# Loading a chunk's r, k and w as 128 rows instead of 96, and zeroing the heads of the 32 extra rows

## The chip, the cores and the metric

One core of a Trainium2 chip. The metric is the device time of one execution in microseconds (us); the kernel before took 305.26 us, the median of three executions (304.26 to 307.01).

## The reference

A recurrent attention over 768 positions (4 batches, 8 heads, head dimension 48) feeds a mixture of experts that uses one of 8 experts per token. Only the first half matters for the change:

```python
for t in range(S):
    cur = einsum('bhd,bhe->bhde', u * k[t], v[t])
    y[t] = einsum('bhd,bhde->bhe', r[t], state + cur)
    state = w[t][:, None] * state + einsum('bhd,bhe->bhde', k[t], v[t])
```

The rows of y, with the heads side by side, go through a skip test, a router (softmax over 8 logits, the best expert taken) and the chosen expert, `relu(x @ w1) @ w2`, times its gate.

## The kernel before

The positions are cut into 24 chunks of 128 (6 for each batch). A chunk works on all 8 heads: a partition holds one dimension of one of two head groups, and the free axis holds four heads of 128 positions each. A group has 48 dimensions, so the data fill 96 of the 128 partitions. Partitions 16 to 63 hold one group, 64 to 111 the other, and 0 to 15 and 112 to 127 hold nothing of the chunk.

A loop over s from -2 to 24 is a software pipeline. In step s PE finishes chunk s (`update`, `outputs`, `rows_out`) and makes the scores of chunk s+1 (`rows_of_keys`, `scores`, `bonus_sums`), DVE scans chunk s+2 (`prep_scan`, `prep_keys`, `prep_reads`) and then masks the scores of chunk s+1 and writes its bonus term into psY (`mask`, L321; `bonus`, L334), and SP issues the loads of chunk s+4. Every engine works through its instructions in the order in which they are written (`manual_schedule`). From step 3 on the experts' weights are loaded as well, and at steps 6, 12 and 18 a router pass is dripped between the DVE instructions.

The buffers of r, k and w (`wrk_sb`) go round in three, those of v transposed (`vt_sb`) in four. A load writes only 96 partitions of a buffer, so the other 32 are set once at the start: w to 1, r and k to 0 (`clear_w`, L201; `clear_rk`, L204). For buffer 0 POOL and DVE do it, for buffers 1 and 2 POOL alone.

The decay is handled by two scans on DVE: q (L266) is the product of w from a position to the end of the chunk, and rh (L288) the product from the start, which begins with a "head", 1/q of the first position. The head is written into a spare column of the w buffer by the reciprocal at L281. Then rp = r * rh (L293), kq = k * q (L283) and rk = r * k (L275). In an empty partition w = 1 and r = k = 0 make all three zero.

The constants come over ACT's DMA queue in `load_chunk(0)`: c_sb, then u_sb in three pieces (`shifted` copies the two groups from the layout of the host to partitions 64, 16 and 0), then the transposed v of chunk 0. After that ACT loads its table and clears psA, sblk and fills ubk_sb (L221 to L231). `rowsk` is 1 in the 96 used partitions and 0 in the others; it is loaded in step 18 on SP's queue, and only a test near the end of the kernel reads it.

Of the kernel before, what the change touches and what calls it, by code (L numbers as in the profile page):

```python
# [8 lines left out]
F32 = mybir.dt.float32  # L9
# [6 lines left out]
ALU = mybir.AluOpType  # L16
# [3 lines left out]
B, H, S, D = 4, 8, 768, 48  # L20
E, DM, DF = 8, 384, 1024
P = 128
# [5 lines left out]
NP = H // 2  # L28
# [12 lines left out]
R_OFF = 1 + NP * CW  # L41
K_OFF = R_OFF + NP * P
V_OFF = K_OFF + NP * P
HP = 64
LO = HP + D
KO = HP - D
# [10 lines left out]
def rwkv_moe_kernel(ctx, tc, wrk, wrk0, vN, uP, wgs, wgp, w12, cst, out):  # L57
    nc = tc.nc
# [6 lines left out]
    n = len(seq)  # L65
# [56 lines left out]
    with tc.tile_pool(name="att", bufs=2) as att, \  # L122
# [6 lines left out]
        def shifted(eng, dst, src):  # L129

            eng.dma_start(dst[HP:], src[HP:])
            eng.dma_start(dst[KO:HP], src[:D])
            eng.dma_start(dst[:KO], src[D:HP])

        def load_chunk(i):
            b, c = seq[i]
            rows = wrk[b, c].rearrange("g d n -> (g d) n")
            t = wrk_sb[i % NBUF]
            vf = vt_sb[i % (NBUF + 1)].rearrange("p a j -> p (a j)")
            if i == 0:  # L140
                nc.sync.dma_start(t[KO:LO, :R_OFF], rows[:, :R_OFF])
                nc.sync.dma_start(t[KO:LO, R_OFF:V_OFF], rows[:, R_OFF:V_OFF])
                nc.scalar.dma_start(c_sb[:, :C_IOTA], cst[:, :C_IOTA])
                shifted(nc.scalar, u_sb, uP)
                nc.scalar.dma_start(vf, wrk0[:, V_OFF:V_OFF + NP * P])
                return
            nc.sync.dma_start(t[KO:LO], rows[:, :V_OFF])
            for g in range(2):
                nc.sync.dma_start(vf[64 * g:64 * g + D], wrk[b, c, g, :, V_OFF:V_OFF + NP * P])

# [6 lines left out]
        c_sb = keep.tile([P, C_W], F32, name="c_sb")  # L157
        ubk_sb = keep.tile([P, NP, P], F32, name="ubk_sb")
        u_sb = pers.tile([P, NP], F32, name="u_sb")
        rowsk = keep.tile([P, 1], F32, name="rowsk")  # L160
        ident = c_sb[:, C_ID:C_ID + P]
        tri = c_sb[:, C_TRI:C_TRI + P]
        iota = keep.tile([P, 2 * P], BF16, name="iota")
# [36 lines left out]
        def clear_w(eng, i):  # L200
            eng.memset(wrk_sb[i][:, :R_OFF], 1.0)  # L201

        def clear_rk(eng, i):
            eng.memset(wrk_sb[i][:, R_OFF:], 0.0)  # L204

        def setup():
            clear_w(nc.gpsimd, 0)
            clear_rk(nc.vector, 0)
            load_chunk(0)
            nc.vector.memset(warm, 0.0)  # L210
            clear_w(nc.gpsimd, 1)
            clear_rk(nc.gpsimd, 1)
            nc.gpsimd.memset(vt_sb[1], 0.0)
            load_chunk(1)
            load_v(0)
            nc.vector.memset(pss, 0.0)
            ints = ones_w.bitcast(U32)
            for a in range(NP):
                at = (a + 1) * CW - 1
                nc.vector.memset(ints[:, at // 4:at // 4 + 1], 1 << 8 * (at % 4))  # L220
            nc.scalar.activation(junk0, warm[:, 0:1], AF.Exp)  # L221
            for z in (*psa, *sblk):
                nc.scalar.copy(z.rearrange(("p a j -> p (a j)", "p a g j -> p (a g j)")
                                           [len(z.shape) - 3]), warm)
            nc.gpsimd.memset(ubk_sb, 0.0)
            clear_w(nc.gpsimd, 2)
            clear_rk(nc.gpsimd, 2)
            nc.gpsimd.memset(vt_sb[2], 0.0)
            for g in range(2):
                rows = slice(64 * g, 64 * g + HP)  # L230
                nc.scalar.copy(ubk_sb[rows, :, rows],  # L231
                               u_sb[rows].rearrange("p (a o) -> p a o", o=1)
                               .to_broadcast([HP, NP, HP]))


            nc.tensor.matmul(psy.rearrange("p a j -> p (a j)"), warm[:, :P], warm,
                             start=True, stop=True, skip_group_check=True)
            nc.tensor.matmul(psu.rearrange("p a j -> p (a j)"), warm[:, :P], warm[:, :NP * HP],
                             start=True, stop=True, skip_group_check=True)
# [38 lines left out]
        def prep_keys(i):  # L278
            wk = work[i]
            heads = wk["w"][:, 0:NP * CW].rearrange("p (a j) -> p a j", a=NP)  # L280
            nc.vector.reciprocal(heads[:, :, 0:1], wk["q"][:, :, 0:1])  # L281
            kq = wk["kq"] = att.tile([P, NP, P], F32, tag="kq", name=f"kq{i}")
            nc.gpsimd.tensor_tensor(kq, wk["k"], wk["q"][:, :, 1:1 + P], op=ALU.mult)  # L283

# [288 lines left out]

        with tc.manual_schedule():
            setup()
            fill(FILL0)
            for s in range(-2, n + 1):
                on = lambda i: 0 <= i < n
                if s + 4 < n:
                    load_chunk(s + 4)  # L580
                if on(s + 3) and s + 3 >= 1:
                    load_v(s + 3)
                if s == -2:
                    nc.sync.dma_start(wgp_sb, wgp)
                if s == 1:
                    nc.sync.dma_start(c_sb[:, C_IOTA:], cst[:, C_IOTA:])
                if s == LATE:
                    nc.sync.dma_start(wgs_sb, wgs)
                    shifted(nc.sync, rowsk, cst[:, C_HS + 2:C_HS + 3])
                if on(s - 1):  # L590
                    store(s - 1)
                for i0, m in GROUPS:
                    if i0 + m == s:
                        pace[0] = 1 if i0 + m < LATE else 2
                        later.append(router(i0, m))
                        if i0 + m == LATE:
                            later.append(early())
                if on(s):
                    update(s)
                    carry(s)  # L600
                if on(s + 2):
                    prep_scan(s + 2)
                drip(pace[0])
                if on(s):
                    outputs(s)
                flush()
                if on(s + 2):
                    prep_keys(s + 2)
                    drip(pace[0])
                    if s != -1:  # L610
                        prep_reads(s + 2)
                if s == -2:
                    bonus_keys(0)
                    nc.gpsimd.memset(vt_sb[3], 0.0)
                    nc.gpsimd.memset(onesb, 1.0)
                    nc.gpsimd.memset(ohs, 0.0)
                    nc.gpsimd.memset(key, 0.5)
                if on(s):
                    evict(s)
                if on(s + 1):  # L620
                    rows_of_keys(s + 1)
                    if s == 0:
                        bonus_sums(1)
                    scores(s + 1)
                    drip(2 * pace[0])
                    mask(s + 1, 0)
                    mask(s + 1, 1)
                    drip(pace[0])
                    if s != 0:
                        bonus_sums(s + 1)  # L630
                    bonus(s + 1)
                if s == -1:
                    prep_reads(1)
                if on(s + 2):
                    prep_check(s + 2)
                for _ in range(min(2, len(marks))):
                    marks.popleft()()
                if s == n - 1:
                    early_tokens(0)
                if on(s):  # L640
                    rows_out(s)
                flush()
                if s in (1, 2, 3):
                    nc.scalar.copy(*((trib, tri), (identb, ident),
                                     (iota, c_sb[:, C_IOTA:C_IOTA + 2 * P]))[s - 1])
                if s == 4:
                    nc.scalar.copy(iotaw, iota.bitcast(F32))
                k = s + 1 - W_AT
                for eq, k0 in (((0, 1), 0), ((1, 0), 9), ((0, 0), 16), ((1, 1), 18)):
                    if k == k0:  # L650
                        gens[eq] = load_weights(*eq)
                    if k0 <= k < k0 + 3:
                        next(gens[eq])
                if 3 <= k < 9:
                    split_slice(0, 3 + k, nc.gpsimd)
                if 12 <= k < 18:
                    split_slice(1, k - 12, nc.gpsimd)
# [40 lines left out]
    with tc.tile_pool(name="wset1", bufs=1) as ws1, tc.tile_pool(name="moe", bufs=2) as moe:  # L698
# [55 lines left out]

        def verdict():
            psf = ps1.tile([P, 512], F32, tag="psT", name="psf", bufs=2)
            nc.tensor.matmul(psf[0:1, 0:1], rowsk, vt[:, 0:1], start=True, stop=False)
            nc.tensor.matmul(psf[0:1, 0:1], rows1_, vt[:, 3:4], start=False, stop=True)
            nc.vector.tensor_scalar(flag_i, psf[0:1, 0:1], 0.0, None, op0=ALU.is_gt)

# [245 lines left out]
```

## Time and profile before

| | |
|---|---|
| median of three executions | 305.26 us (304.26 to 307.01) |
| the profiled execution | 304.25 us, of which the span from first to last instruction is 302.5 us |
| PE busy | 289.8 us, 96% of the span |
| DVE, ACT, POOL busy | 216.8, 176.2, 141.3 us |
| mean granted TensorE clock | 0.995 |
| loads of r, k, w after the first chunk | 23 of 579.4 KB |

The profile is of one execution. The DMA share of a stretch is the mean busy share of the 16 DMA engines; a value of 1 or a little more means that they always had a packet in hand.

### The profile page before, as it was taken

What the parts mean: (1) busy time and instruction counts of PE and PEld (TensorE: products, weight loads), DVE (VectorE), ACT (ScalarE), POOL (GpSimd) and SP (SyncE); (2) the same over time, 40 slices, a digit from 0 to 9 for tenths busy, and PEclk for the clock granted to TensorE, in tenths of its full rate; (3) what the DMA queues carried; (4) which work ended last, traced back from release to release, by engine and by line L of the source; (5) the groups of instructions that cost most, each with busy time, mean ns of one, the idle gap of its engine ahead of it and who ended that gap; (6) DMA issues with size and microseconds to landing.
All of it is one profiled execution on the core that took longest, in us unless ns stands there. A gap on an engine that the chain in (4) does not pass through costs nothing.

```text
span 302.5 us, 8272 instructions
## 1 busy us (share of the span) xinstructions
PE 289.8 (96%) x3228; PEld 269.3 (89%) x3228; DVE 216.8 (72%) x410; ACT 176.2 (58%) x493; POOL 141.3 (47%) x140
## 2 busy tenths in 40 slices
PE   6799999999999999899999999999999999999993
PEld 2689889889888988799899999999999999999992
DVE  5987779877888787976253879693967859496320
ACT  5284645799577986797433666391846638184310
POOL 7795665978976589766106771302011020201101
PEclk9999999999999999999999999999999999999998
DMA  6999999999799967765513699746266563630001
GB/s 189 261 243 262 286 282 245 237 249 223 194 289 265 284 181 225 191 224 165 176 72 89 195 378 362 254 168 229 101 226 227 208 250 103 246 117 26 9 2 40
DMA packets 22737, 60.28 MB, mean 199 GB/s; under 512 B 3926, under 2 KB 10490, under 8 KB 22688
## 3 DMA queue, kind: packets, MB, share of 16 engines
q1 hardware_dynamic: 20176, 53.79, 60.5%
q0 software_dynamic: 2048, 5.48, 5.5%
q8 instruction: 27, 0.44, 0.6%
q10 hardware_dynamic: 464, 0.40, 0.6%
q14 instruction: 22, 0.18, 0.2%
HBM read 52.60 MB, written 7.86 MB: 200 GB/s over the span
## 4 chain that ended last, share of the span: by engine, by line
issue 32%; PE 23%; DVE 5%; POOL 5%; DMA 4%; ACT 1%; POOLq 1%; SPq 0%; DVEq 0%
POOL out L728 5%; PE psY L370 3%; PE psY L365 3%; PE psB L330 3%; PE psA L315 3%; PE psX L381 2%; PE psH L115 2%; DMA vt<-wrk 2%; DMA v<-vN 1%; PE psu L344 1%; DMA xg<-out,idr 1%; DVE psY L334 1%; PE psH L792 1%; PE psH L791 1%; PE psH L790 1%
## 5 line engine op out<-in xcount | busy, mean ns | idle before, releaser
L728 POOL DMA_INDIRECT out<-fin,ids x16 | 17.1, 1070 | 100.9 <-DVE fin L823 94.4
L797 ACT ACTIVATE hh<-psH 128x256 fp32r<-128x256 f32 x60 | 23.1, 384 | 56.8 <-PE psH L792 53.8
L792 PE MATMUL psH<-xTh,w1l 128*128 128x256 f32 x168 | 47.5, 283 | 0.0
L791 PE MATMUL psH<-xTl,w1h 128*128 128x256 f32 x168 | 47.5, 283 | 0.0
L790 PE MATMUL psH<-xTh,w1h 128*128 128x256 f32 x168 | 47.5, 283 | 0.0
L321 DVE TENSOR_TENSOR asb<-psA,c_sb 128x512 f32<-128x512 f32 x48 | 30.8, 684 | 17.0 <-PE psA L315 17.0
L814 PE MATMUL psO<-w2h,hh 128*128 128x384 f32 x120 | 40.9, 341 | 0.0
L816 PE MATMUL psO<-w2h,hl 128*128 128x384 f32 x120 | 40.2, 335 | 0.0
L815 PE MATMUL psO<-w2l,hh 128*128 128x384 f32 x120 | 40.1, 334 | 0.0
L802 DVE SCALAR_TENSOR_TENSOR hl<-psH,hh 128x256 fp32r<-128x256 f32 x60 | 25.2, 421 | 12.3 <-ACT hh L797 12.0
L275 POOL TENSOR_TENSOR rk<-wrk 128x512 f32<-128x512 f32 x24 | 30.9, 1287 | 6.2 <-POOL rp L293 2.5
L288 DVE TENSOR_TENSOR_SCAN rh<-wrk,pss 128x520 f32<-128x520 f32 x24 | 29.7, 1235 | 4.2 <-PE pss L498 2.4
L792 PEld LDWEIGHTS psH<-xTh,w1l 128*128 128x128 f32 x168 | 32.2, 192 | 0.0
L791 PEld LDWEIGHTS psH<-xTl,w1h 128*128 128x128 f32 x168 | 32.2, 192 | 0.0
L790 PEld LDWEIGHTS psH<-xTh,w1h 128*128 128x128 f32 x168 | 32.2, 191 | 0.0
L293 POOL TENSOR_TENSOR rp<-wrk,rh 128x512 f32<-128x512 f32 x23 | 27.2, 1182 | 9.8 <-DVE rh L288 7.9
L283 POOL TENSOR_TENSOR kq<-wrk,q 128x512 f32<-128x512 f32 x24 | 28.3, 1179 | 7.3 <-DVE q L266 5.9
L266 DVE TENSOR_TENSOR_SCAN q<-wrk,pss 128x520 f32<-128x520 f32 x24 | 29.3, 1222 | 2.0 <-DMA wrk<-wrk 1.9
L90 DVE TENSOR_TENSOR w2l<-r,w2h 128x512 fp32r<-128x512 f32 x42 | 27.8, 687 | 1.0
L365 PE MATMUL psY<-asb,v 128*48 128x128 f32 x384 | 26.6, 276 | 1.8 <-DVE psY L334 1.3
L89 ACT CAST w2h<-r 128x512 fp32r<-128x512 f32 x48 | 27.9, 626 | 0.4 <-DMA r<-w 0.4
L330 PE MATMUL psB<-rk,ubk_sb 128*128 128x128 f32 x192 | 27.7, 287 | 0.0
(148 smaller groups left out, 633.7 us busy)
## 6 DMA issues: line engine op xcount, KB each, us to landing
r<-w SPq DMA_DIRECT2D x48, 512.0 KB, 5.4
wrk<-wrk SPq DMA_DIRECT2D x23, 579.4 KB, 7.0
v<-vN SPq DMA_DIRECT2D x24, 192.0 KB, 5.6
out<-x SPq DMA_DIRECT2D x24, 192.0 KB, 4.9
vt<-wrk SPq DMA_DIRECT2D x46, 96.0 KB, 6.4
wrk<-wrk SPq DMA_DIRECT2D x1, 384.0 KB, 4.7
vt<-wrk ACTq DMA_DIRECT2D x1, 256.0 KB, 7.7
out<-fin,ids POOLq DMA_INDIRECT x16, 4.1
```

The source lines that it names most:

```text
L275: nc.gpsimd.tensor_tensor(work[i]["rk"].rearrange("p a j -> p (a j)"), t[:, R_OFF:K_OFF], t[:, K_OFF:V_OFF], op=ALU.mult)
L288: nc.vector.tensor_tensor_scan(rh.rearrange("p a j -> p (a j)"), wk["w"][:, 0:NP * CW], ones_at[:, :NP * CW], 1.0, op0=ALU.mult, op1=ALU.max)
L321: nc.vector.tensor_tensor(s, psa[g], tri.rearrange("p (o j) -> p o j", o=1).to_broadcast([P, NP, P]), op=ALU.mult)
L330: nc.tensor.matmul(wk["psb"][:, a], ubk_sb[:, a], wk["rk"][:, a], start=True, stop=True)
L365: nc.tensor.matmul(psy[64 * g:64 * g + D, a], v[:, 2 * a + g], wk["asb"][g][:, a], start=False, stop=(c == 0), skip_group_check=True)
L728: sc = nc.gpsimd.indirect_dma_start(out=out, out_offset=bass.IndirectOffsetOnAxis(ap=ids[:, s % 2, s // 2:s // 2 + 1], axis=0), in_=o, in_ ...
L790: nc.tensor.matmul(ps, w1h[:, o:o + P], xTh[:, kc], start=(kc == 0), stop=False)
L791: nc.tensor.matmul(ps, w1h[:, o:o + P], xTl[:, kc], start=False, stop=False)
L792: nc.tensor.matmul(ps, w1l[:, o:o + P], xTh[:, kc], start=False, stop=(kc == KC - 1))
L814: nc.tensor.matmul(pso, h[j, fc][0], w2h[:, o], start=(fc == 0), stop=False)
L815: nc.tensor.matmul(pso, h[j, fc][0], w2l[:, o], start=False, stop=False)
L816: nc.tensor.matmul(pso, h[j, fc][1], w2h[:, o], start=False, stop=(fc == FC - 1))
```

## The change

The rows of all chunks lie one after another in DRAM, so the load of chunk i, for i from 1 to 22, now takes 128 rows that start 16 rows before its own: the 32 outer partitions receive the neighbours' r, k and w. Chunks 0 and 23 still load 96 rows. Since every partition of buffers 1 and 2 is now written by a load, their four memsets on POOL are gone; buffer 0 is still cleared, as its first load is of 96 rows.

What the neighbours' rows would do is stopped at one place: after the reciprocal the heads are multiplied by rowsk, so that the scan rh is zero in the outer partitions, and rp with it. For this the reciprocal of chunks 1 to 23 goes to a small tile `hd`, and a DVE multiplication writes hd * rowsk into the head column. rowsk has to be there early: its three pieces are loaded on ACT's queue, between u_sb and the transposed v of chunk 0, and no longer on SP's in step 18.

```diff
         def load_chunk(i):
             b, c = seq[i]
-            rows = wrk[b, c].rearrange("g d n -> (g d) n")
+            rows = wrk.rearrange("b c g d n -> (b c g d) n")
+            at = 2 * D * i
...
             if i == 0:
-                nc.sync.dma_start(t[KO:LO, :R_OFF], rows[:, :R_OFF])
-                nc.sync.dma_start(t[KO:LO, R_OFF:V_OFF], rows[:, R_OFF:V_OFF])
+                nc.sync.dma_start(t[KO:LO, :R_OFF], rows[:2 * D, :R_OFF])
+                nc.sync.dma_start(t[KO:LO, R_OFF:V_OFF], rows[:2 * D, R_OFF:V_OFF])
                 nc.scalar.dma_start(c_sb[:, :C_IOTA], cst[:, :C_IOTA])
                 shifted(nc.scalar, u_sb, uP)
+                shifted(nc.scalar, rowsk[:, 0], cst[:, C_HS + 2:C_HS + 3])
                 nc.scalar.dma_start(vf, wrk0[:, V_OFF:V_OFF + NP * P])
                 return
-            nc.sync.dma_start(t[KO:LO], rows[:, :V_OFF])
+            if i < n - 1:
+                nc.sync.dma_start(t, rows[at - KO:at - KO + P, :V_OFF])
+            else:
+                nc.sync.dma_start(t[KO:LO], rows[at:at + 2 * D, :V_OFF])
...
             nc.vector.memset(warm, 0.0)
-            clear_w(nc.gpsimd, 1)
-            clear_rk(nc.gpsimd, 1)
             nc.gpsimd.memset(vt_sb[1], 0.0)
...
             nc.gpsimd.memset(ubk_sb, 0.0)
-            clear_w(nc.gpsimd, 2)
-            clear_rk(nc.gpsimd, 2)
             nc.gpsimd.memset(vt_sb[2], 0.0)
...
         def prep_keys(i):
...
-            nc.vector.reciprocal(heads[:, :, 0:1], wk["q"][:, :, 0:1])
+            hd = att.tile([P, NP, 1], F32, tag="hd", name=f"hd{i}") if i > 0 else heads[:, :, 0:1]
+            nc.vector.reciprocal(hd, wk["q"][:, :, 0:1])
+            if i > 0:
+                nc.vector.tensor_tensor(heads[:, :, 0:1], hd, rowsk.to_broadcast([P, NP, 1]),
+                                        op=ALU.mult)
...
                 if s == LATE:
                     nc.sync.dma_start(wgs_sb, wgs)
-                    shifted(nc.sync, rowsk, cst[:, C_HS + 2:C_HS + 3])
```

## Rows read from the trace of the kernel before

**Rows 1.** The page: busy time of the engines, share of the span, instructions.

```profile
PE 289.8 (96%) x3228; PEld 269.3 (89%) x3228; DVE 216.8 (72%) x410; ACT 176.2 (58%) x493; POOL 141.3 (47%) x140
```

**Rows 2.** Stretches of 6 us: each engine's busy time, then clock, DMA share, GB/s.

```profile
6.00:12.00 6.00, 3.67 (x49) 2.47 (x47) 5.86 (x8) 2.57 (x7) 5.17 (x8) 1.00 1.03 244
12.00:18.00 6.00, 5.37 (x87) 4.56 (x86) 5.93 (x9) 3.19 (x12) 4.10 (x5) 1.00 1.05 255
24.00:30.00 6.00, 6.00 (x95) 5.38 (x93) 4.47 (x7) 3.77 (x13) 3.90 (x4) 1.00 1.03 263
```

**Rows 3.** DVE and PE in order of time at the start: start, us, what, [idle before].

```profile
10.94 1.16 PE L330 MATMUL psB<-rk,ubk_sb 128*128 128x128 f32 x8
...
12.33 0.69 DVE L334 TENSOR_TENSOR psY<-psB,vt 128x512 f32<-128x512 f32 x1
...
14.10 1.24 DVE L266 TENSOR_TENSOR_SCAN q<-wrk,pss 128x520 f32<-128x520 f32 x1
...
15.37 0.18 DVE L281 RECIPROCAL wrk<-q 128x4 f32<-128x4 f32 x1
15.58 1.24 DVE L288 TENSOR_TENSOR_SCAN rh<-wrk,pss 128x520 f32<-128x520 f32 x1
...
17.93 0.69 DVE L334 TENSOR_TENSOR psY<-psB,vt 128x512 f32<-128x512 f32 x1
...
18.67 1.08 PE L365 MATMUL psY<-asb,v 128*48 128x128 f32 x16
```

**Rows 4.** Who waited for whom: us in total, times, longest; PE's rows.

```profile
PE psY L365 <- DVE psY L334: 1.3, 2, 0.9
...
PEld psY L365 <- DVE psY L334: 2.9, 8, 1.0
```

**Rows 5.** PE's weight loads in order of time, columns as in rows 3.

```profile
53.17 0.82 PEld L365 LDWEIGHTS psY<-asb,v 128*48 128x48 f32 x16 [0.26 <-DVE psY L334]
...
124.48 0.83 PEld L365 LDWEIGHTS psY<-asb,v 128*48 128x48 f32 x16 [1.02 <-DVE psY L334]
```

**Rows 6.** DVE in a later step, columns as in rows 3.

```profile
28.34 1.29 DVE L321 TENSOR_TENSOR asb<-psA,c_sb 128x512 f32<-128x512 f32 x2 [1.39 <-PE psA L315]
```

**Rows 7.** ACT and its queue in order of time.

```profile
2.37 0.44 ACTq L133 DMA_DIRECT2D u_sb<-uP  x1
2.85 0.44 ACTq L145 DMA_DIRECT2D vt<-wrk  x1
3.32 1.28 ACT L221 ACT_TABLE_LOAD   x1 [3.32 <-issue]
...
7.05 0.83 ACT L231 COPY ubk_sb<-u_sb 64x256 f32<-64x256 f32 x2 [0.17 <-DMA u_sb<-uP]
```

**Rows 8.** What SP's queue waited for up to 24 us: total us, times, longest.

```profile
SPq L149 <- DMA u_sb<-uP: 1.4, 1, 1.4
...
SPq L584 <- DMA vt<-wrk: 1.1, 1, 1.1
```

**Rows 9.** First DMA issues (up to 3.1 us): KB each, us from issue to landing.

```profile
wrk<-wrk SPq DMA_DIRECT2D x1, 579.4 KB, 6.5
...
vt<-wrk ACTq DMA_DIRECT2D x1, 256.0 KB, 7.7
...
u_sb<-uP ACTq DMA_DIRECT2D x1, 0.2 KB, 4.6
```

**Rows 10.** SP's queue in order of time.

```profile
5.76 0.37 SPq L147 DMA_DIRECT2D wrk<-wrk  x1
```

**Rows 11.** The same load among the DMA issues, columns as in rows 9.

```profile
wrk<-wrk SPq DMA_DIRECT2D x1, 579.4 KB, 8.2
```

**Rows 12.** Two short stretches, columns as in rows 2.

```profile
10.20:11.60 1.40, 1.40 (x37) 1.23 (x27) 1.37 (x3) 0.00 (x0) 1.40 (x2) 1.00 1.03 245
...
174.00:176.00 2.00, 2.00 (x18) 2.00 (x17) 0.81 (x2) 0.60 (x2) 1.13 (x2) 1.00 1.04 417
```

**Rows 13.** POOL's first work on data.

```profile
6.83 1.18 POOL L283 TENSOR_TENSOR kq<-wrk,q 128x512 f32<-128x512 f32 x1 [1.43 <-DVE wrk L281]
```

More of the change, by code (lines that the diff above doesn't have):

```diff
@@ L159, in rwkv_moe_kernel @@
         u_sb = pers.tile([P, NP], F32, name="u_sb")
-        rowsk = keep.tile([P, 1], F32, name="rowsk")
+        rowsk = keep.tile([P, 1, 1], F32, name="rowsk")
         ident = c_sb[:, C_ID:C_ID + P]
@@ L756, in verdict @@
             psf = ps1.tile([P, 512], F32, tag="psT", name="psf", bufs=2)
-            nc.tensor.matmul(psf[0:1, 0:1], rowsk, vt[:, 0:1], start=True, stop=False)
+            nc.tensor.matmul(psf[0:1, 0:1], rowsk[:, 0], vt[:, 0:1], start=True, stop=False)
             nc.tensor.matmul(psf[0:1, 0:1], rows1_, vt[:, 3:4], start=False, stop=True)
```

## Prediction

> **What bounds the kernel now.** The page comes first: PE is busy 96% of the span [rows 1], so what can be won or lost lies where PE stands still, or in what makes it stand still. The stretches of 6 us show where that is: between 6 and 18 us PE works 3.67 and 5.37 of 6 us, from 24 us on all of it, and in the same early stretches DVE is busy for 5.86 and 5.93 of 6 us while the DMA engines show a share of 1.03 to 1.05 [rows 2]. So up to about 19 us DVE sets the time, with the DMA engines full beside it; after that PE does. The order in time confirms it: from the bonus of chunk 0 at 12.33 us to that of chunk 1 at 17.93 us DVE goes from one instruction straight to the next, and PE's outputs of chunk 1 start at 18.67 us, as that bonus ends (17.93 + 0.69) [rows 3]. In the list of waits PE's weight loads wait for psY of DVE in only 8 of 24 chunks, 2.9 us in all, of which 1.3 us stand as idle time of the matmuls [rows 4]. Three of the 8 belong to steps with a router pass (53.17, 88.32 and 124.48 us, the first and the last shown) [rows 5]; an ordinary step has 1.39 us of room on DVE before the masks [rows 6]. A delay of PE's start is never won back, since PE has no idle time left to give.
>
> **The part that DVE gets: 23 multiplications.** The row is the reciprocal of the same 128x4 shape, 0.18 us; with its result waited for, the next instruction starts 0.21 us after it (15.37 to 15.58) [rows 3]. I take 0.2 us each. They come behind the first scan and before the second and the masks. In most steps they fall into the 1.39 us before the masks [rows 6] and cost nothing; if that cover were gone, all 23 would cost 4.6 us. They lie on the path where DVE does: in chunks 1 and 2 at the start, each 0.2 us, and in the three steps with a router pass, where PE already waits for the bonus [rows 5]. Of the other five waits [rows 4] one is chunk 0's and counted, and four (0.22 us each) are at the ends of the batches, where the masks themselves wait for PE. That gives 5 x 0.2 = 1.0 us. From below the bound is 0, if the extra instruction fits into the stalls between dependent small ones.
>
> **The part that ACT's queue gets: three more loads ahead of chunk 0's v.** From one issue of the pieces of u_sb to the next are 0.48 us (2.37 to 2.85), so their issue costs about 1.4 us. ACT now issues v at 2.85 us (done 3.29), loads its table at 3.32 and has filled ubk_sb at 7.88, 4.6 us after the last issue [rows 7]. ubk_sb is first read by PE's bonus sums at 10.94 [rows 3], and the bonus behind them may start 0.4 us later than the sums allow now (12.10 to 12.33, and 0.2 for the multiplication). So ACT may slip by 3.1 + 0.4 = 3.5 us before PE notices, and 1.4 us of issue alone are free.
>
> What is not free is a wait that the queue may meet. In the trace a transfer is issued only when an earlier, unrelated one has landed: SP's load of vt waits 1.4 us for a piece of u_sb, its load of wgp 1.1 us for chunk 0's vt [rows 8], which lands at 2.85 + 7.7 = 10.6 us [rows 7, 9]. Matched in order of issue, each waits for the one eight issues before it, SP's and ACT's counted together. Now the first eight end with ACT's last load, so ACT meets no such wait; with three more, chunk 0's v becomes about the 14th or 15th and waits for the 6th or 7th. The 6th is u_sb's last piece, landing at 2.37 + 4.6 = 7.0 us; the 7th is chunk 1's load, issued at 2.4 us now that no memset holds it, landing 6.5 us later at 8.9 [rows 7, 9], or about 8 if 128 rows move faster (below) and chunk 0's v no longer travels among them. Behind this waiting issue stand, on ACT, the table load, the clears of psA and ubk_sb. ACT would be free at 7.4 us (4.1 late, cost 0.6), at 8.4 (5.1 late, cost 1.6), or at 9.3 (cost 2.5); with no wait at all at 4.7 (cost 0). I take 1.0 us, between the first two, because the 6th and the 7th are issued almost together, and keep 0 and 2.5. The data of that v would land at 7.0 + about 5 us or a little later, close to the 12.5 us at which the bonus needs it.
>
> **The part that the DMA engines get.** 22 loads grow from 579.4 KB to 772.5 KB. Cover is thin at the start: chunk 2's load is issued at 5.76 and lands 8.2 us later, at 13.96, and the scan that needs it starts at 14.10 [rows 3, 10, 11]. The price has two ends. While that load is on its way the engines are full at 245 GB/s; at that rate 32 rows more take 198 kB / 245 = 0.81 us. Between 174 and 176 us, where only the experts' weights move, all of them into 128 partitions, the engines are as full at 417 GB/s [rows 12]; at that rate the whole load of 128 rows takes 791 / 417 = 1.9 us against 593 / 245 = 2.4 us now, 0.5 us less. I take the second row as the nearer one, since it has the shape that the change makes, and count 0: loads that land earlier than now gain nothing, because DVE, not the landing, sets these scans.
>
> [...]
>
> **What goes away.** Four memsets on POOL: POOL's first work on data waits 1.43 us for DVE with them in place [rows 13], so 0. Chunk 1's load leaves 0.3 us earlier; its scan follows DVE's rp of chunk 0, so 0. SP's three issues in step 18: the loads there are for three steps ahead, so 0.
>
> **Sum.** 1.0 (DVE) + 1.0 (ACT) + 0 (DMA) + 0 (removed) = 2.0 us. The profiled execution took 304.25 us, so 306.2 us. That execution lay 1.0 us below the median of the runs shown, 305.26; against the median it is 307.2 us, 0.65% slower.
>
> **Rivals.** (a) ACT meets no wait, or only a short one: 0 to 0.2 + 1.0 us, about 306.4. For it: none of ACT's issues waits in this trace. Against it: SP's do. (b) ACT's v stands a place or two later and waits for chunk 1's load or the vt behind it at 9 us or more: 2.5 to 3.4 + 1.0 us, 308.8 to 309.7; it decides from the point at which ACT is free after 9 us, for then PE's scores of chunk 0 wait for psA too. (c) The 128 rows are no faster than the 96: 0.81 us more for each chunk while the engines are full. Chunk 2 lands 1.6 us late and chunk 3 2.4 us late, with 1.4 us of room on DVE from then on; with the weights' loads in steps 3 to 5 it makes 2.5 to 4 us on top of the sum, 309.7 to 311. For it: the early stretches are full. Against it: the weights' rate. (d) The engines' relief is worth something: with loads landing 0.5 us earlier the start and the router steps lose their idle time of 1.3 us and the multiplication hides: 304.0 to 305. For it only the thin cover of chunk 2; against it, that DVE is not seen waiting for a landing after its first scan. That the change doesn't do what it says would be rows that don't arrive as one transfer on 16 engines; then (c) holds.
>
> **How the numbers follow.** Forecast 0.50 (306.0 to 308.3), (a) 0.20, (b) 0.13, (c) 0.10, (d) 0.07. A measurement of this kernel tells about 1% (3.05 us) from no change. Slower by more is (b) and (c) for the most part and the top of the forecast: 0.24. Faster by more would take 302.2 us, which no term gives: 0.04. Within: 0.72. The range leaves out the lower half of (d) and the upper part of (c): 304.8 to 309.8.
>
> **What would show it.** A multiplication of about 0.2 us behind each reciprocal; ACT's table load at 7 us or later, behind an issue that waits for a landing; bonus sums of chunk 0 later than 10.94 and outputs of chunk 1 at 19.5 to 21 instead of 18.67, with the same distance kept to the end; a DMA share below 1 in the early stretches, and landings of wrk in under 7 us. Table load before 5 us: (a). Scans of chunks 2 to 4 that wait for wrk: (c). I would be wrong if the start kept its time and a later stage moved.

## The result and the profile after

The changed kernel takes 309.79 us (median of four executions, 309.42 to 310.88) against 305.48 us of the kernel before beside it: a ratio of 1.0133, with an interval of 1.0090 to 1.0177. It is slower by 4.3 us, more than twice the 2.0 us of the forecast. The profiled execution took 309.86 us with a span of 307.9 us, 5.4 us more than the span before.

The page of the changed kernel, busy time by engine: PE's work is the same as in [rows 1], DVE has 18.2 us more.

```profile
PE 290.5 (94%) x3228; PEld 269.5 (88%) x3228; DVE 235.0 (76%) x433; ACT 176.8 (57%) x493; POOL 138.5 (45%) x136
```

23 instructions more for 18.2 us are 0.8 us each, and the one line that was added shows it (durations are the smallest, the median and the largest in ns):

```profile
L285 DVE TENSOR_TENSOR wrk<-hd,rowsk x23: 166/1029/1231, 11.6 to 143.0; 128x4 f32<-128x4 f32 x23
```

DVE, then POOL, in an ordinary step, in order of time (start, duration):

```profile
28.19 1.03 DVE L285 TENSOR_TENSOR wrk<-hd,rowsk 128x4 f32<-128x4 f32 x1
...
30.89 1.29 DVE L326 TENSOR_TENSOR asb<-psA,c_sb 128x512 f32<-128x512 f32 x2 [0.33 <-PE psA L320]
```

```profile
28.02 1.18 POOL L288 TENSOR_TENSOR kq<-wrk,q 128x512 f32<-128x512 f32 x1 [0.53 <-DVE q L267]
```

The multiplication of 512 numbers starts while POOL's kq is running and ends at 29.22, 0.02 us after kq ends at 29.20. So it is with all of them: 21 of the 23 end 0.02 us after the POOL instruction beside them, be it kq, rk or work on the experts' weights, and last as long as that one has left; the two that last 0.17 us began in the last 0.13 us of one. The room before the masks has gone from 1.39 us [rows 6] to 0.33 us: in an ordinary step the multiplication is hidden even so. Where there is no room it is not. The first chunks, as in [rows 3]:

```profile
10.13 1.24 DVE L267 TENSOR_TENSOR_SCAN q<-wrk,pss 128x520 f32<-128x520 f32 x1 [1.23 <-DMA wrk<-wrk]
...
11.61 1.04 DVE L285 TENSOR_TENSOR wrk<-hd,rowsk 128x4 f32<-128x4 f32 x1
12.57 1.27 DVE L326 TENSOR_TENSOR asb<-psA,c_sb 128x512 f32<-128x512 f32 x2
13.76 0.68 DVE L339 TENSOR_TENSOR psY<-psB,vt 128x512 f32<-128x512 f32 x1
...
16.96 1.15 DVE L285 TENSOR_TENSOR wrk<-hd,rowsk 128x4 f32<-128x4 f32 x1
...
20.48 0.69 DVE L339 TENSOR_TENSOR psY<-psB,vt 128x512 f32<-128x512 f32 x1
```

```profile
21.22 1.08 PE L370 MATMUL psY<-asb,v 128*48 128x128 f32 x16 [1.14 <-DVE psY L339]
...
129.41 1.08 PE L370 MATMUL psY<-asb,v 128*48 128x128 f32 x16 [0.90 <-DVE psY L339]
...
135.87 1.08 PE L370 MATMUL psY<-asb,v 128*48 128x128 f32 x16 [0.27 <-DVE psY L339]
```

The bonus of chunk 0 is 1.43 us late (13.76 against 12.33): 0.43 us because the scan of chunk 1 waits for its load, and 1.0 us for the multiplication. The bonus of chunk 1 is 2.55 us late: one multiplication more. PE's outputs follow: chunk 1 at 21.22 instead of 18.67 us, chunk 19 at 129.41 instead of 124.48 [rows 3, 5], and after chunk 20 (5.46 us late) the distance stays. So 2.55 us are lost up to chunk 1 and 2.9 us at the steps with a router pass. The waits of PE for psY (us in all, times, longest) have grown from 1.3 and 2.9 us [rows 4]:

```profile
PEld psY L370 <- DVE psY L339: 7.1, 10, 1.6
...
PE psY L370 <- DVE psY L339: 5.5, 6, 1.4
```

ACT's queue, as in [rows 7]:

```profile
4.62 0.32 ACTq L133 DMA_DIRECT2D rowsk<-cst  x1
6.91 0.35 ACTq L147 DMA_DIRECT2D vt<-wrk  x1
7.30 1.28 ACT L224 ACT_TABLE_LOAD   x1 [7.30 <-DMA u_sb<-uP]
...
10.77 0.81 ACT L232 COPY ubk_sb<-u_sb 64x256 f32<-64x256 f32 x2
```

Chunk 0's v leaves at 6.91 us, when a piece of u_sb has landed, and the table load follows. ubk_sb is ready at 11.58, so PE's bonus sums start late, at 11.72 instead of 10.94 us; but the bonus behind them is held until 13.76 by DVE itself, so this wait is not seen in the end. The stretches of [rows 2] again (us, then busy us by engine, granted clock, DMA share, GB/s):

```profile
6.00:12.00 6.00, 3.33 (x43) 1.95 (x41) 4.67 (x5) 4.66 (x11) 4.91 (x8) 1.00 0.78 208
12.00:18.00 6.00, 4.95 (x84) 4.24 (x82) 5.93 (x8) 2.60 (x10) 2.96 (x3) 1.00 1.01 359
24.00:30.00 6.00, 6.00 (x104) 5.37 (x98) 5.83 (x8) 3.88 (x15) 3.61 (x3) 1.00 1.03 328
```

PE does less by 18 us, at a full clock. The engines now move 359 GB/s in the second stretch; the load of chunk 1 lands 7.6 us after its issue.

### The profile page after: what moved, and what is told of

Its sections match the earlier page's. It is cut to its first block, busy times and chain, and to the rows that moved or that the text cites. A ratio compares the mean times of both kernels' runs of the same rounds, so it can differ in the third digit from the quotient of the medians.

```text
span 307.9 us, 8288 instructions
## 1 busy us (share of the span) xinstructions
PE 290.5 (94%) x3228; PEld 269.5 (88%) x3228; DVE 235.0 (76%) x433; ACT 176.8 (57%) x493; POOL 138.5 (45%) x136
## 4 chain that ended last, share of the span: by engine, by line
issue 31%; PE 23%; DVE 5%; POOL 5%; DMA 4%; ACT 1%; POOLq 1%; SPq 0%; DVEq 0%
POOL out L732 5%; PE psY L375 3%; PE psY L370 3%; PE psB L335 3%; PE psA L320 3%; PE psX L386 2%; PE psH L115 2%; DMA vt<-wrk 1%; DMA v<-vN 1%; DMA xg<-out,idr 1%; PE psu L349 1%; DVE psY L339 1%; PE psH L796 1%; PE psH L795 1%; PE psH L794 1%
## 5 line engine op out<-in xcount | busy, mean ns | idle before, releaser
L827 DVE SCALAR_TENSOR_TENSOR fin<-psO,gates,xg 128x384 f32<-128x384 f32 x15 | 9.3, 618 | 25.6 <-PE psO L820 25.3
```

## The experiments

The theory that this trace suggests: the multiplication itself should last 0.16 us, and stands still until POOL's instruction beside it is over, because both of its operands lie in SBUF (A in the expectations). The rivals: the loads of 128 rows cost the time (C); the loads on ACT's queue do; an added step between the two scans costs it, however short. Each kernel is told by its outputs of chunk 1 and of chunk 19 in the profiled execution: the first holds the loss of the start, the difference that of the steps behind it.

The first can be set side by side only where PE's clock was the same. In the traces of 5, 7 and 11 the granted clock was 0.50 in a stretch between 12 and 17 us, in that of 8 it was 0.60 and 0.55 from 14.20 to 18.20 us. Its mean over the span was 0.991 to 0.994 in these four and in 6, 10 and 12, and 0.995 to 1.000 in all others. The difference begins behind these stretches and is free of them.

| kernel | multiplication, median us | outputs of chunk 1 | of chunk 19 | difference | median, before beside it (us) | ratio, interval |
|---|---|---|---|---|---|---|
| before | none | 18.67 | 124.48 | 105.81 | | |
| changed | 1.03 | 21.22 | 129.41 | 108.19 | 309.79, 305.48 | 1.0133, 1.0090 to 1.0177 |
| 1 loads alone | none | 18.86 | 124.67 | 105.81 | 304.95, 306.33 | 0.9982, 0.9943 to 1.0021 |
| 2 without the multiplication | none | 18.96 | 124.77 | 105.81 | 304.95, 306.33 | 0.9974, 0.9940 to 1.0009 |
| 3 ACT's loads alone | none | 19.34 | 125.25 | 105.91 | 304.97, 306.33 | 0.9944, 0.9913 to 0.9974 |
| 4 multiplication, 96 rows | 1.03 | 21.04 | 129.22 | 108.18 | 309.22, 304.45 | 1.0114, 1.0024 to 1.0205 |
| 5 kq behind it | 0.17 | 20.87 | 127.18 | 106.31 | 308.06, 304.45 | 1.0087, 1.0048 to 1.0127 |
| 6 operand copied to PSUM | 0.16 | 21.45 | 128.29 | 106.84 | 308.94, 304.45 | 1.0121, 1.0026 to 1.0215 |
| 7 operand set in PSUM, loads late | 0.16 | 21.26 | 128.10 | 106.84 | 306.93, 306.33 | 1.0023, 0.9988 to 1.0057 |
| 8 the same again | 0.16 | 21.39 | 128.24 | 106.85 | 306.29, 305.33 | 1.0034, 1.0001 to 1.0067 |
| 9 operand set in PSUM, loads early | 0.16 | 19.29 | 126.13 | 106.84 | 308.19, 306.17 | 1.0085, 1.0051 to 1.0120 |
| 10 scalar operand | 1.04 | 22.29 | 131.25 | 108.96 | 311.74, 304.45 | 1.0201, 1.0109 to 1.0292 |
| 11 times a constant | 1.04 | 21.83 | 130.15 | 108.32 | 311.16, 305.33 | 1.0208, 1.0160 to 1.0256 |
| 12 on ACT | 0.30 | 19.91 | 131.79 | 111.88 | 313.38, 305.33 | 1.0274, 1.0232 to 1.0316 |

### Which part of the change costs the time

**1, the loads alone** (to the changed kernel):

```diff
-                shifted(nc.scalar, rowsk[:, 0], cst[:, C_HS + 2:C_HS + 3])
...
-            nc.vector.reciprocal(hd, wk["q"][:, :, 0:1])
-            if i > 0:
-                nc.vector.tensor_tensor(heads[:, :, 0:1], hd, rowsk.to_broadcast([P, NP, 1]),
-                                        op=ALU.mult)
+            nc.vector.reciprocal(heads[:, :, 0:1], wk["q"][:, :, 0:1])
...
+                    shifted(nc.sync, rowsk[:, 0], cst[:, C_HS + 2:C_HS + 3])
```

> The changed kernel without the multiplication and without the three early loads on ACT: 128-row loads and no clears of later buffers alone, heads are left unmultiplied, so the rows of the neighbours take part in the sums. Theory A (the multiplication beside POOL's work carries the loss): outputs of chunk 1 at 18.2 to 19.2 us, of chunk 19 at 124 to 125.5 us, ratio to before 0.995 to 1.004. Theory C (128-row loads carry it): outputs of chunk 19 at 127.5 us or later, ratio 1.008 or more. If relief of the DMA engines is worth something that the multiplication hid, chunk 19 comes before 124.0 us and the ratio is under 0.995.

```profile
18.86 1.08 PE L365 MATMUL psY<-asb,v 128*48 128x128 f32 x16 [0.17 <-DVE psY L334]
...
124.67 1.08 PE L365 MATMUL psY<-asb,v 128*48 128x128 f32 x16 [0.90 <-DVE psY L334]
```

The outputs of chunk 1 start at 18.86 us, and the 105.81 us from there to chunk 19 are those of the kernel before, to the hundredth. The loads of 128 rows cost no more than the 0.19 us of the start, and their relief of the engines is worth nothing that shows either.

**2, without the multiplication**: the same edit, with the three loads left on ACT's queue.

> The changed kernel without the multiplication alone (the three early loads stay on ACT; heads are left unmultiplied, so the rows of the neighbours take part in the sums). Theory A: vf0's issue at 6.9 us or later, bonus sums 0.5 to 2 us later than in the kernel before, and this now shows, since no multiplication hides it: outputs of chunk 1 at 19.2 to 21.5 us, of chunk 19 at 125 to 127 us, ratio 1.002 to 1.008. Rival (ACT's loads cost nothing): the same as with the loads on SP late, outputs of chunk 1 within 0.3 us of that kernel.

```profile
18.96 1.08 PE L366 MATMUL psY<-asb,v 128*48 128x128 f32 x16 [0.29 <-DVE psY L335]
...
124.77 1.08 PE L366 MATMUL psY<-asb,v 128*48 128x128 f32 x16 [0.90 <-DVE psY L335]
```

The issue of chunk 0's v is at 6.36 us, the table load at 6.75 and the bonus sums at 11.18, 0.24 us later than before; outputs of chunk 1 come at 18.96 and again 105.81 us before those of chunk 19. The expected 19.2 to 21.5 us was missed: ACT is 3.4 us late, within the 3.5 us of slack that the prediction had worked out. Against experiment 1 the early loads cost 0.1 us here and nothing in the median.

**3, ACT's loads alone** (to the kernel before):

```diff
                 shifted(nc.scalar, u_sb, uP)
+                shifted(nc.scalar, rowsk[:, 0], cst[:, C_HS + 2:C_HS + 3])
...
-                    shifted(nc.sync, rowsk, cst[:, C_HS + 2:C_HS + 3])
```

> The kernel before, with the three loads of the vector of ones and zeros early on ACT instead of late on SP, and nothing else. My prediction's term of ACT: vf0's issue waits for the landing of the eighth DMA before it, at 6.9 to 8.4 us, outputs of chunk 1 0.4 to 2 us later (19.1 to 20.7 us), the time 0.4 to 2 us longer, ratio 1.001 to 1.007. Rival (ACT's queue has room, nothing waits): outputs of chunk 1 at 18.7 us, ratio 1.000 within 0.002.

Outputs of chunk 1 are at 19.34 us, 0.67 us late, but not by ACT: the bonus of chunk 0 starts at 12.37 us, as before. SP's queue, then DVE:

```profile
9.75 0.31 SPq L148 DMA_DIRECT2D wrk<-wrk  x1
```

```profile
14.77 1.24 DVE L267 TENSOR_TENSOR_SCAN q<-wrk,pss 128x520 f32<-128x520 f32 x1 [0.58 <-ACT psu L354]
```

Chunk 2's load is issued at 9.75 us instead of 5.76 [rows 10], right after chunk 1's load has landed (9.69), eight issues before it on the two queues together; it lands at 14.65, and the scan starts behind it at 14.77 instead of 14.10 (the row names ACT's psu instead, but in the trace of before this scan starts at 14.10, ahead of that step's psu at 14.39). So the three issues push a wait onto SP's queue that the prediction had looked for on ACT's alone. In the time none of it is seen: the ratio is below 1, and the expected 1.001 to 1.007 was missed. That goes with the clock, not with the kernel: all ten executions of this one had a mean granted clock of 0.995 or more and took 304.4 to 305.3 us, but only 17 of the 35 of the kernel before beside it, which took 303.8 to 306.7 us (median 305.3); the other 18 took 305.7 to 308.8. A ratio here that differs from 1 by half a per cent can be the clock's.

**4, the multiplication with loads of 96 rows and the clears** (to the changed kernel):

```diff
-            rows = wrk.rearrange("b c g d n -> (b c g d) n")
-            at = 2 * D * i
+            rows = wrk[b, c].rearrange("g d n -> (g d) n")
...
-            if i < n - 1:
-                nc.sync.dma_start(t, rows[at - KO:at - KO + P, :V_OFF])
-            else:
-                nc.sync.dma_start(t[KO:LO], rows[at:at + 2 * D, :V_OFF])
+            nc.sync.dma_start(t[KO:LO], rows[:, :V_OFF])
...
+            clear_w(nc.gpsimd, 1)
+            clear_rk(nc.gpsimd, 1)
...
+            clear_w(nc.gpsimd, 2)
+            clear_rk(nc.gpsimd, 2)
```

> The kernel before (loads of 96 rows, all clears) with only the multiplication by rowsk added, and rowsk loaded on ACT's queue as in the change. Theory A: the multiplications take about 1.0 us, as POOL's kq runs beside them whatever the loads are; the total is that of the changed kernel less what the 128-row loads cost at the start (0.4 us): 309 to 310. Rival C (the 128-row loads carry the loss): 306 to 307.

```profile
L285 DVE TENSOR_TENSOR wrk<-hd,rowsk x23: 166/1029/1243, 11.4 to 142.8; 128x4 f32<-128x4 f32 x23
```

Chunk 1 at 21.04, the difference 108.18: nearly the whole loss stands without the 128 rows. With 1 and 2, from the other side, that settles the part: it is the multiplication.

### Why it lasts 1.03 us

**5, POOL's kq waits for the multiplication** (to the changed kernel):

```diff
-                nc.vector.tensor_tensor(heads[:, :, 0:1], hd, rowsk.to_broadcast([P, NP, 1]),
-                                        op=ALU.mult)
+                mul = nc.vector.tensor_tensor(heads[:, :, 0:1], hd, rowsk.to_broadcast([P, NP, 1]),
+                                              op=ALU.mult)
...
+                tc.add_manual_dep(ga.ins, mul.ins.name,
+                                  mybir.DependencyInfo(mybir.DependencyClass.Sync,
+                                                       mybir.DependencyReason.DATA),
+                                  reason="port")
```

> The changed kernel, but POOL's kq of chunks 1 to 23 waits for the multiplication, so that the two no longer overlap. Theory A: multiplications of about 0.2 us wherever no other POOL operation (rk, w1l, w2l) runs, kq about 0.4 us later without anybody waiting for it in ordinary steps; 306.5 to 308. Theory B: 1.0 us each and later than the changed kernel, 310 to 311.

DVE's multiplication, POOL's kq behind it, and an early chunk where POOL is at rk instead (DVE, POOL):

```profile
27.84 0.17 DVE L285 TENSOR_TENSOR wrk<-hd,rowsk 128x4 f32<-128x4 f32 x1
```

```profile
28.15 1.18 POOL L288 TENSOR_TENSOR kq<-wrk,q 128x512 f32<-128x512 f32 x1 [1.16 <-DVE wrk L285]
```

```profile
16.61 1.15 DVE L285 TENSOR_TENSOR wrk<-hd,rowsk 128x4 f32<-128x4 f32 x1
```

```profile
16.45 1.29 POOL L276 TENSOR_TENSOR rk<-wrk 128x512 f32<-128x512 f32 x1
```

With POOL idle the same instruction takes 0.17 us; with rk beside it, it ends at 17.76, 0.02 us after rk (17.74). The difference falls to 106.31 us. Chunk 1 stays at 20.87, but of its two multiplications, which still stand beside rk, only the second can have held it up. The bonus of chunk 0 waits 1.31 us more for PE's sums, which start late behind ACT's queue (at 11.43 us) and run at a granted clock of 0.50 (DVE, then a stretch with the columns as above):

```profile
13.40 0.70 DVE L344 TENSOR_TENSOR psY<-psB,vt 128x512 f32<-128x512 f32 x1 [1.31 <-PE psB L340]
```

```profile
12.00:14.00 2.00, 2.00 (x22) 1.77 (x21) 0.69 (x2) 0.09 (x1) 0.15 (x1) 0.50 1.06 316
```

The time, 308.06 us, is just above the expected 306.5 to 308.

**6, the second operand copied to PSUM by ACT** (to the changed kernel):

```diff
+        rowsp = scratch(1).rearrange("p (a o) -> p a o", a=1)
...
+            if i == 1:
+                nc.scalar.copy(rowsp, rowsk)
...
-                nc.vector.tensor_tensor(heads[:, :, 0:1], hd, rowsk.to_broadcast([P, NP, 1]),
+                nc.vector.tensor_tensor(heads[:, :, 0:1], hd, rowsp.to_broadcast([P, NP, 1]),
```

> The changed kernel, but rowsk is copied once to PSUM (by ACT, before chunk 1's reciprocal) and the tensor_tensor reads it there: same operation, shape, broadcast and destination, one input in SBUF. Theory A: 0.1 to 0.2 us each and 306.5 to 307.5, as with the scalar. Theory B: unchanged at 1.0 us each, 309.5 to 310.

```profile
L288 DVE TENSOR_TENSOR wrk<-hd,pss x23: 161/163/164, 13.4 to 142.8; 128x4 f32<-128x4 f32 x23
```

All 23 last 0.16 us, with POOL's kq running as in the changed kernel, and the difference falls to 106.84 us. The time, 308.94 us, missed the expected 306.5 to 307.5. The start pays for ACT: the first multiplication waits 2.11 us for the copy, in ACT's queue behind a table load at 8.75 us, which came behind the landing of a piece of rowsk:

```profile
13.45 0.16 DVE L288 TENSOR_TENSOR wrk<-hd,pss 128x4 f32<-128x4 f32 x1 [2.11 <-ACT pss L283]
```

```profile
8.75 1.28 ACT L225 ACT_TABLE_LOAD   x1 [8.75 <-DMA rowsk<-cst]
```

**7, the operand set in PSUM by DVE, the loads of rowsk late on SP** (to the changed kernel):

```diff
-                shifted(nc.scalar, rowsk[:, 0], cst[:, C_HS + 2:C_HS + 3])
...
+        rowsp = scratch(1).rearrange("p (a o) -> p a o", a=1)
...
+            for lo, hi, one in ((0, P, 1.0), (0, KO, 0.0), (96, P, 0.0), (96, LO, 1.0)):
+                nc.vector.memset(rowsp[lo:hi], one)
...
-                nc.vector.tensor_tensor(heads[:, :, 0:1], hd, rowsk.to_broadcast([P, NP, 1]),
+                nc.vector.tensor_tensor(heads[:, :, 0:1], hd, rowsp.to_broadcast([P, NP, 1]),
...
+                    shifted(nc.sync, rowsk[:, 0], cst[:, C_HS + 2:C_HS + 3])
```

> The changed kernel, with the vector of ones and zeros set in PSUM by four small memsets on DVE at the start, read there by the multiplication, and its three loads put back on SP late, so that ACT has its old queue again. Theory A (the multiplication stands still while POOL works, because both of its inputs lie in SBUF; ACT's three loads cost nothing behind that but cost at the start once it is gone): all 23 multiplications 0.15 to 0.2 us, vf0's issue on ACT near 6.2 us, outputs of chunk 1 at 18.7 to 20 us and of chunk 19 at 124.5 to 126 us (before: 18.67 and 124.48), ratio to before 0.998 to 1.006. Theory B (a further operation of DVE per chunk costs this, whatever it lasts): ratio 1.010 or more, chunk 19 at 128 us or later. Theory C (the loads of 128 rows cost it): ratio 1.010 or more with multiplications of 0.2 us and longer waits for wrk.

The difference is 106.84 us again, but chunk 1 is at 21.26. The stretches around PE's outputs of chunk 0 (columns as above):

```profile
12.00:14.20 2.20, 0.32 (x12) 0.19 (x7) 2.13 (x5) 0.00 (x0) 1.04 (x1) 0.94 1.04 298
14.20:16.10 1.90, 1.88 (x17) 1.50 (x17) 1.90 (x2) 0.73 (x4) 0.72 (x1) 0.50 1.00 360
16.10:18.20 2.10, 2.10 (x18) 1.98 (x16) 1.90 (x4) 1.97 (x7) 2.10 (x3) 0.70 0.93 204
```

```profile
14.22 1.95 PE L372 MATMUL psY<-asb,v 128*48 128x128 f32 x16 [1.90 <-DVE psY L341]
```

Chunk 1's load landed at 10.53 us (9.15 in the trace of before), the scan behind it held up the masks and the bonus of chunk 0, PE stood still for 1.90 us, and as it went on the granted clock was 0.50: the 16 outputs took 1.95 us instead of 1.08. So chunks 1 and 19 come later than theory A said (18.7 to 20 and 124.5 to 126 us). The time, 306.93 against 306.33, is that of the kernel before within 0.6%, as A said.

**8, the same kernel once more.**

> The kernel with its multiplier set in PSUM once more, for its first 20 us: there the load of chunk 1 landed at 10.53 us, PE stood still for 1.90 us and then ran at a granted clock of 0.50. If that was chance of the DMA engines, the landing is at 9.4 to 10.1 us this time, no stretch is at 0.50, outputs of chunk 1 come at 19.0 to 19.8 us and those of chunk 19 again 106.8 us after them. If it belongs to the kernel, the first 20 us repeat: outputs of chunk 1 at 21.0 to 21.5 us.

The start repeated itself: the load landed at 10.51, PE stood still for 1.51 us, and the clock was 0.60 and 0.55 in the two stretches from 14.20 to 18.20 us. In experiment 11, whose queues are the same, the load landed at 10.51 too. In experiment 1, again with these queues, it landed at 9.76 and in 12 at 9.36, so the order of issues alone does not set it; what does stays open. Nor do the two traces tell how the kernel mostly starts. They are of executions of 307.85 and 307.93 us, the latter the longest of its ten; six of those ten had a mean granted clock of 0.996 or more and took 304.75 to 306.48 us, and no trace shows their start.

**9, the operand set in PSUM, the loads of rowsk early on ACT** (as 7, without its first and its last hunk; to the changed kernel nothing differs but where the multiplier lies).

> The changed kernel with one thing altered: the multiplication reads its ones and zeros from PSUM, where four small memsets on DVE put them at the start; the three early loads stay on ACT. Theory A (1.03 us of standing still per multiplication is the loss, and an operand in PSUM ends it): multiplications of 0.16 us, outputs of chunk 19 minus those of chunk 1 at 106.8 us (changed kernel 108.19, without the multiplication 105.81), outputs of chunk 1 at 19.2 to 20 us as without the multiplication (18.96) plus 0.2 and what the mask has to wait, ratio to before 1.001 to 1.007. Rival (a further step in the chain from scan to scan costs what the changed kernel lost, whatever its length): chunk 1 at 21 us or later and 108 us from there to chunk 19, ratio 1.010 or more. If chunk 1 is again at 21.0 to 21.5 us with the load of chunk 1 landing by 9.8 us, the start has a cause of its own that neither of the two names.

PE's bonus sums, DVE's bonus, and PE's outputs of chunks 1 and 19:

```profile
11.64 1.13 PE L338 MATMUL psB<-rk,ubk_sb 128*128 128x128 f32 x8 [0.80 <-ACT ubk_sb L235]
...
19.29 1.08 PE L373 MATMUL psY<-asb,v 128*48 128x128 f32 x16 [0.15 <-DVE psY L342]
...
126.13 1.08 PE L373 MATMUL psY<-asb,v 128*48 128x128 f32 x16 [0.90 <-DVE psY L342]
```

```profile
12.81 0.70 DVE L342 TENSOR_TENSOR psY<-psB,vt 128x512 f32<-128x512 f32 x1 [0.56 <-PE psB L338]
```

With the multiplication at 0.16 us, chunk 1 is 0.62 us late and chunk 19 1.65 us; the span is 304.5 us, 2.0 us over that of before, against 5.4 us for the changed kernel. Experiment 2, without the multiplication, had a span of 302.9 us. The mean granted clock of these four traces is 0.995 to 0.997. So in single executions 0.4 of the 5.4 us are there without a multiplication, 1.6 us go with one that does not stand still (0.33 of them at the start, where ACT's queue was later than in 2), and 3.4 us with the standing still. Part of the 3.4 is that chunk 1's load landed at 9.17 us here and at 10.11 in the changed kernel. So the rival is right in part: an added step costs something even at 0.16 us.

The times say the same less sharply. The medians are 308.19 and 306.17, 2.0 us apart, for the changed kernel 4.3; the ratio of 0.85% lies above the expected 1.001 to 1.007, and its interval overlaps that of the changed kernel. The trace of experiment 7 shows a later start than this one, though its times have a smaller ratio; but the two traces are from opposite ends, this one of the shortest of twelve executions (307.03 us), that one of an execution above its kernel's median. Besides, some 0.6 us of this kernel's time lie outside the span (time less span: median 2.4 us, 1.8 for the kernel before).

### Which form of operation stands still

**10, the multiplication as one with a scalar operand** (to the changed kernel):

```diff
-                nc.vector.tensor_tensor(heads[:, :, 0:1], hd, rowsk.to_broadcast([P, NP, 1]),
-                                        op=ALU.mult)
+                nc.vector.tensor_scalar(heads[:, :, 0:1], hd, rowsk[:, 0], None, op0=ALU.mult)
```

> The changed kernel, but the head's mask is a per-partition scalar: tensor_scalar reads one tensor from SBUF and takes rowsk as the scalar, where tensor_tensor read two tensors. Theory A (the multiplication, 0.17 us by itself, stands still until the kq product that POOL has begun is over, because both read through something that DVE needs for a second input): each multiplication 0.1 to 0.2 us, in the trace it no longer ends with kq; the start's outputs of chunk 1 about 19.8 us instead of 21.2; total 306.5 to 307.5. Theory B (the operation is slow in itself, by its broadcast, its strided destination or its dependence on the reciprocal): still 1.0 us each, 309.5 to 310.

**11, times the constant 1.0** (the same line, the loads of rowsk late on SP):

```diff
+                nc.vector.tensor_scalar(heads[:, :, 0:1], hd, 1.0, None, op0=ALU.mult)
```

> The changed kernel with a multiplication by the constant 1.0 in the place of the one by ones and zeros (so one operand in SBUF instead of two; the heads of the neighbours' rows are not zeroed), and the three loads back on SP late. Theory A (it is the second operand in SBUF that makes the operation stand still beside POOL): 23 operations of 0.15 to 0.2 us, outputs of chunk 19 minus those of chunk 1 at 106.6 to 107.2 us as with the operand in PSUM (106.84; before 105.81; the changed kernel 108.19), ratio to before 1.002 to 1.007. Rival (any DVE operation at this place, right beside POOL's kq, stands still): operations of 1 us and chunk 19 minus chunk 1 at 108 us, ratio 1.009 or more.

The added line of 10 and of 11:

```profile
L285 DVE TENSOR_SCALAR wrk<-hd,rowsk x23: 232/1037/1231, 11.2 to 144.9; 128x4 f32<-128x4 f32 x23
```

```profile
L284 DVE TENSOR_SCALAR wrk<-hd x23: 172/1035/1249, 12.0 to 143.8; 128x4 f32<-128x4 f32 x23
```

Both stand still as the changed kernel's does, the second with one operand in SBUF and no other. The time of 10, 311.74 us, is above what either theory said, with ACT's v leaving only at 8.09 us and a mean granted clock of 0.991. So the second operand is not what makes it; that part of the theory falls. What 6, 7 and 9 have is an operand in PSUM. And the reciprocal, with its one operand and its result in SBUF, takes 0.18 us at most in all 24 chunks of the changed kernel, some of them inside a POOL instruction (51.86 to 52.03 within kq from 51.29 to 52.47): not every operation on SBUF alone is held. Why the multiplication by a constant is held (1.04 us) and the reciprocal is not is not shown.

### Another engine

**12, the multiplication on ACT** (to the changed kernel; rowsk is set by four memsets on DVE, as rowsp in 7, and none of its loads is left):

```diff
-                nc.vector.tensor_tensor(heads[:, :, 0:1], hd, rowsk.to_broadcast([P, NP, 1]),
-                                        op=ALU.mult)
+                nc.scalar.mul(heads[:, :, 0], hd[:, :, 0], rowsk[:, 0])
```

> The changed kernel with the multiplication on ACT (a copy scaled by the vector of ones and zeros, which four memsets on DVE set at the start; none of its three loads is left). Theory A with DVE as the engine that carries the loss: outputs of chunk 19 minus those of chunk 1 at 105.8 to 106.2 us, the time at that of the kernel before, ratio 0.996 to 1.002. Rival (the added step in the chain from scan to scan costs it, on whatever engine): ACT's operation and two handovers stand between reciprocal and rh, chunk 19 minus chunk 1 at 107.5 us or more, ratio 1.006 or more. The first chunks can be late by the ACT queue: outputs of chunk 1 at 18.7 to 20 us.

ACT's order and DVE's rh in an ordinary step, and the waits of rh for ACT (us in all, times, longest):

```profile
26.21 1.20 ACT L358 ACTIVATE psu<-psu,q 128x48 f32<-128x48 f32 x4
27.44 0.64 ACT L363 COPY sblk<-psu 64x192 f32<-64x192 f32 x2
28.10 0.30 ACT L286 ACTIVATE wrk<-hd,rowsk 128x4 f32<-128x4 f32 x1
```

```profile
28.50 1.24 DVE L293 TENSOR_TENSOR_SCAN rh<-wrk,pss 128x520 f32<-128x520 f32 x1 [1.66 <-ACT wrk L286]
```

```profile
DVE rh L293 <- ACT wrk L286: 16.2, 13, 2.3
```

The rival that an added step in the chain of the two scans costs it holds here: the result is there at 26.85, ACT comes to it at 28.10 behind the state's update, and rh waits 1.66 us. The difference is 111.88 us, the worst of all. Of all kernels only number 3, which has neither the loads of 128 rows nor a multiplication, is measured below the kernel before clear of its interval, by 0.6%; nothing in its trace shows a gain, and the clock accounts for it, as said there. No version that keeps the change's work beats the kernel before.

## Why the forecast was too low

The time of 309.79 us lies just inside the range that was stated, 304.8 to 309.8 us. That is luck: the upper end of the range came from the rivals (b) and (c), and the runs bear out neither.

**What bounds the kernel** held. The time is lost up to chunk 1 and at the steps with a router pass, and what PE loses there is not won back: 5.46 us at chunk 20, 5.4 us at the end. In an ordinary step the multiplication stays hidden, even at 1.03 us: 1.39 - 1.03 = 0.36 us, and the masks still wait 0.33 us.

**The part that DVE gets** is the step that failed, by the size of one term: "I take 0.2 us each". The five places were right, but the multiplication lasts 1.04 and 1.15 us in the two at the start (chunks 1 and 2), and 0.43, 1.15 and twice 0.88 us in the three steps with a router pass (chunks 8, 14, 20 and, one more, 21). There PE's outputs fell behind by 1.0, 1.12, 0.55, 1.32, 0.51 and 0.53 us, 5.0 us together, where five times 0.2, 1.0 us, had been put; with the 0.43 us of chunk 1's load they are the 5.46 us at chunk 20. The 0.2 us were too little even for a multiplication that is not held: in experiments 6 to 9 it costs 1.03 us between chunks 1 and 19 (106.84 - 105.81), where three times 0.2 us had been put. Why a step of 0.16 us costs twice that there is not shown. The reciprocal was the wrong row: same shape, same place, but not the same operands. The trace of before had a nearer one, DVE's rp of chunk 0, with POOL's rk beside it (DVE, POOL):

```profile
8.00 1.78 DVE L293 TENSOR_TENSOR rp<-wrk,rh 128x512 f32<-128x512 f32 x1
```

```profile
7.96 1.27 POOL L275 TENSOR_TENSOR rk<-wrk 128x512 f32<-128x512 f32 x1
```

It takes 1.78 us, where the bonus of the same shape takes 0.69 [rows 3]: 0.55 us after rk's end at 9.23 it is done. It is also the only instruction of two inputs on DVE's path up to 19 us that has both in SBUF; the scans, the masks and the bonus each read one from PSUM. As an upper bound, a POOL instruction's 1.2 us would have given 5 x 1.2 = 6 us, 5 us more than was put.

**The part that ACT's queue gets** was right in its mechanism and too large in its size. The v load did wait for the landing of a piece of u_sb (6.91 us; 7.0 was worked out), the table load came at 7.30 (7.4), the bonus sums at 11.72. In the changed kernel the multiplication hides that. Where nothing hides it, the slack of 3.5 us that was worked out shows: ACT 3.4 us late costs the bonus of chunk 0 nothing (12.34 us in experiment 2, 12.33 before), ACT 3.9 us late costs it 0.48 us (12.81 in 9). What the prediction missed is SP's queue: the same three issues make chunk 2's load wait for chunk 1's landing (experiment 3, and 10.12 us in the changed kernel).

**The part that the DMA engines get** was right at 0 from chunk 1 on: 105.81 us with 96 rows and with 128. The one exception is the load of chunk 1, which landed at 10.11 us instead of 9.15 and is worth 0.43 us at the start. That it is the 128 rows is not shown: loads of 96 rows landed at 9.69 us (3) and 9.86 us (4), loads of 128 rows anywhere from 8.2 us (5) to 10.5 us (7). Rival (c) is refuted by experiment 1, rival (d) too: the relief is there, since the engines move 359 GB/s, but nobody waits for it. **What goes away** was 0, but not as worked out: chunk 1's load left 0.18 us earlier (2.49 us, before 2.67), and its scan then waited 1.23 us for the load and not for rp. The forecast of "outputs of chunk 1 at 19.5 to 21" was missed narrowly (21.22 us), "with the same distance kept to the end" widely: the distance grew from 2.55 to 5.46 us.

## What to carry to other kernels

Before an operation is added to DVE, look at what POOL does at that place, and price it by a row with the same kind of operands (both in SBUF, or one in PSUM), not the same shape: here 0.16 us and 1.03 us are the same multiplication. The multiplication that both engines' order set beside a large instruction of POOL lasted until that one was over, 0.02 us past its end in 21 of 23 cases; one operand in PSUM (0.16 us), or an order in which POOL waits (0.17 us), freed it here. And three tiny loads on one queue held up the next large load on another, which left at 9.75 us instead of 5.76: count issues over both queues.

## What the runs showed of the hardware

The holding works both ways. In experiment 9 DVE's rp of chunk 0 starts first, and POOL's rk, the instruction that takes 1.27 us in the trace of before, takes 1.72 us:

```profile
7.47 0.69 DVE L301 TENSOR_TENSOR rp<-wrk,rh 128x512 f32<-128x512 f32 x1
```

```profile
7.57 1.72 POOL L279 TENSOR_TENSOR rk<-wrk 128x512 f32<-128x512 f32 x1
```

Where rk starts first, in the traces of before and of the changed kernel, it takes 1.27 and 1.26 us, and rp 1.78 and 1.64 us: rp ends 0.55 and 0.56 us after it. In 1, 2, 3 and 7 rp takes 1.51 to 1.65 us too, in 6 and 10 it takes 0.80 and 0.85 us.

PE's granted clock was 0.50 when PE went on after 1.90 us of standing still in the start of experiment 7, and the 16 outputs alone took 0.87 us more. In experiment 4 PE stood still for 1.48 us at the same place and went on at the full clock (mean 1.000); what brings it down is not shown.
